# A third buffer for raw keys and queries, the fourth pair's first head placed by ScalarE, and the routing's preparations taken in turns

## The chip, the core and the metric

The kernel runs on one core of a Trainium2 chip. Its engines are TensorE (PE, with its weight loads PEld), VectorE (DVE), ScalarE (ACT) and GpSimd (POOL); SyncE (SP) issues most transfers, ScalarE some, GpSimd the gathers and scatters. Each engine works off its own list of instructions in order, and waits on semaphores for the others. The metric is device time in microseconds. The kernel before takes 926.87 us (median of 3 runs, 924.33 to 928.79).

## The reference

Causal attention with a bias over 64 heads (batch 8, 8 heads, 576 positions, head size 64), and a two-level mixture of experts on its output (4608 tokens, 4 groups of 4 experts, 512 to 1024 to 512):

```python
scores = np.matmul(q, k.transpose(0, 1, 3, 2)) / np.sqrt(D)
cum = np.cumsum(np.maximum(s, 0.0), axis=-1)
bias = -(cum[:, :, :, None] - cum[:, :, None, :])
scores = np.where(causal, -1e9, scores + np.minimum(bias, 0.0))
attn = softmax(scores)                    # over the keys
x = (attn @ v), heads joined: [4608, 512]
# then: the best group by x @ w_group, in it the best expert by x @ w_expert,
# out = (group weight * expert weight) * (relu(x @ w1) @ w2), for the tokens of each expert
```

## The kernel before

The heads are taken in 32 pairs p; a step is one head. `load_raw(p)` brings the pair's keys and queries (128 partitions by 2 by 576 floats) into a tile r of the pool raw, which has two buffers. Products are made of high and low parts: `split(p, part)` lets ScalarE copy a part of r to hl[:, part], rounded, and GpSimd subtract it from r (L155), which gives the low part. Two tiles feed TensorE. WA[p % 4] holds the high parts of both heads in rows 0 to 63, two rows of the running sum (ch or cumd), and two rows of the row maximum; WB[p % 5] holds the mixed high and low parts. Most of both is filled by transfers inside the core's memory, from hl: `load_a` (WA) and `load_b` (WB) issue them on SP. `place(p, part)` instead lets ScalarE copy straight from r: part 0 puts the first head into WA, parts 1 and 2 put two blocks into WB, and `load_a`/`load_b` with placed=True leave these transfers out. The kernel before places so for pairs 0 to 2 only.

A step runs, interleaved by an order written out by hand (`ORDER0`, `FIRST`, `ORDERS`), the row maxima of the head four steps on (A items, `rowmax`: TensorE pm, VectorE L221), the scores of its own head (B items: TensorE ps, then ScalarE's exponential L279), and the product with the values of the head before (C items: po). The scores go through a ring of three PSUM tiles, so the fourth B item waits for the exponential of the first. Letters in the order pop a queue: b is an exponential, e GpSimd's causal cut (L288), a the maximum, T and t the transposed maxima (VectorE makes th and tl, L241 and L242), D `send`, in which ScalarE issues two small transfers of th and tl into WA (L247). R calls `Router.step`, which runs the next piece of a generator in `rt.queue`, or counts down a wait that the generator yielded. The scores of pair p need the D of that pair, which comes a pair of steps before.

Before step 0 the calls are written out one after another (L456 to L514), and `pre` adds calls at the end of steps -2 to 1. From step 1 on each odd step ends with `load_a` four pairs on, `load_b` three, `load_v` one and `load_raw` six. TensorE, VectorE, ScalarE and GpSimd keep the order in which the code calls them; SP's transfers are put in order by the scheduler after step 0. Each transfer takes one of eight completion counters in turn (DMAHW0 to DMAHW7 in the instruction lists), over the queues of SP and ScalarE together, and its issue waits until the one that held its counter before, eight places ahead, has landed.

`Router.operands` (L672) makes constants for the routing: 4 memsets on GpSimd, 8 casts and small operations on VectorE. In the kernel before it is called at once at the end of step -1, so these stand between the row maxima of step -1 and those of step 0.

After attention come the lists of tokens by expert and the experts' matrix products (`moe`), whose instructions read the attention's output.

Of the kernel before, what the change touches and what calls it, by code (L numbers as in the profile page):

```python
# [8 lines left out]
F32 = mybir.dt.float32  # L9
# [10 lines left out]
B, H, S, D = 8, 8, 576, 64  # L20
P = 128
# [86 lines left out]
def attention(tc, qk, v, s, wr, xs, st):  # L108
# [3 lines left out]
    with ExitStack() as ctx:  # L112

        raw = ctx.enter_context(tc.tile_pool(name="raw", bufs=2))
# [25 lines left out]
            nc.gpsimd.memset(t[64:P, PC[4]:PC[4] + 64], 0.0)  # L140
        hls, raws = {}, {}
        def load_raw(p):
            raws[p] = raw.tile([P, 2, S], F32, name=f"r{p}", tag="r", bufs=2)
            nc.sync.dma_start(raws[p], qk[p])

        def split(p, part, later=False):

            if part == 0:
                hls[p] = raw.tile([P, 3, S], F32R, name=f"hl{p}", tag="hl", bufs=3)
            hl, r = hls[p], raws[p]  # L150
            nc.scalar.copy(hl[:, part], r[:, part])  # L151

            def low(h):
                hr = slice(0, P) if part else slice(h * 64, h * 64 + 64)
                (nc.vector if p < 1 else nc.gpsimd).tensor_tensor(  # L155
                    out=hl[:, 2] if part else WB[p % NBB][0:64, KA, h], in0=r[hr, part],
                    in1=hl[hr, part].bitcast(F32), op=ALU.subtract)

            for h in range(1 if part else 2):
                if later:  # L160
                    push("G", p, lambda h=h: low(h))
                else:
                    low(h)
# [267 lines left out]
        def need(k, i):  # L431

            while fifo[k] and fifo[k][0][0] <= i:
                pop(k)
# [22 lines left out]
        s0, r1, c2 = (c1[:BH, i * S:(i + 1) * S].bitcast(F32) for i in range(3))  # L457
        cumd = dr.tile([BH, 2, S], F32, name="cumd")
        nc.sync.dma_start(s0, s.rearrange("b h s -> (b h) s"))
        load_raw(0)  # L460
        load_raw(1)
        wr_f = ac.tile([P, 4, 20], F32, name="wr_f")
        wr_sb = ac.tile([P, 4, 40], F32R, name="wr_sb")
        nc.scalar.dma_start(wr_f, wr.rearrange("(c p) n -> p c n", p=P))
# [21 lines left out]
        XT = [ac.tile([P, 5 * 64], F32, name=f"xtl{i}") for i in range(2)]  # L486
# [8 lines left out]
        load_a(0, True)  # L495
        split(1, 0)
        split(1, 1)
        load_raw(2)
        place(0, 1)
        place(0, 2)  # L500
        place(1, 0)
# [2 lines left out]
        rt = Router(tc, ac, late, end, small, ring, wr_f, wr_sb, xs, st)  # L504
# [8 lines left out]
        for t in VT:  # L513
# [2 lines left out]

        pre = {-2: [(load_a, 2, True), (load_raw, 3), (load_v, 0)],
               -1: [(load_b, 1, True), (load_raw, 4)],
               0: [(split, 3, 0), (split, 3, 1), (load_a, 3), (load_v, 1)],
               1: [(split, 4, 0), (split, 4, 1), (load_b, 2, True), (load_raw, 5)]}  # L520
        vals, sums, pts = {}, {}, {}

# [12 lines left out]
        for step in range(-LEAD, NH + 5):  # L535
            m, a = step + LEAD, step - 1
            A = rowmax(m) if m < NH else []
            Bq, C = [], []
            if 0 <= step < NH:
                need("T", step // 2)  # L540
                need("t", step // 2)
                need("D", step // 2)
                pts[step] = PT[step % 2]
                Bq = scores(step, pts[step])
            if 0 <= a < NH:
                p = a // 2
                for k in "be":
                    need(k, a)
                if a % 2 == 0:
                    for k in "YZWK":  # L550
                        need(k, p - 2)
                    vals[p] = sm.tile([P, S], F32, name=f"vals{p}", tag="vals", bufs=2)
                    sums[p] = sm.tile([P, S], F32, name=f"sums{p}", tag="sums", bufs=2)
                C = av(a, pts.pop(a), vals[p], sums[p])
            if step >= 2 and step // 2 + 4 < NP:
                push("S", step // 2 + 4, lambda p=step // 2 + 4, part=step % 2: split(p, part, True))
            named = {"A": A, "B": Bq, "C": C}
            order = FIRST if step < 3 else ORDERS if step < NH - 1 else LAST
            for part in order[step % 2] if step > 0 else ORDER0:
                if part[0] in named:  # L560
                    for f in named[part[0]][int(part[1]):int(part[1]) + 1]:
                        f()
                elif part == "R":
                    rt.step(rt.done >= B - 2)
                elif part == "J":
                    if rt.done >= B - 2:
                        rt.step(True)
                else:
                    pop(part)
            for f, *args in pre.get(step, ()):  # L570
                f(*args)
            if step == -1:
                nc.sync.dma_start(cumd, cumh.bitcast(F32))
                rt.operands(XT)
            if step == 62:
                manual.close()
                manual.enter_context(tc.manual_schedule(engines={ENG.PE}))
            if step == 0:
                manual.close()
                manual.enter_context(tc.manual_schedule(engines={ENG.PE, ENG.DVE, ENG.Activation, ENG.Pool}))  # L580
            if step % 2 == 1 and 0 < step < NH:
                for f, lead in ((load_a, 4), (load_b, 3), (load_v, 1), (load_raw, 6)):
                    if step // 2 + lead < NP and (f != load_v or step > 1):
                        need("S", step // 2 + lead)
                        if f in (load_b, load_raw):
                            need("G", step // 2 + lead - 2 * (f == load_raw))
                        f(step // 2 + lead)
        for _ in range(3):
            for k in fifo:
                keep(k, 0)  # L590
# [37 lines left out]
class Router:  # L628


    def __init__(self, tc, ac, sm, end, ps_t, ps_s, wr_f, wr_sb, xs, st):
        self.end = end
        self.tc, self.sm, self.ps_t, self.ps_s, self.xs, self.st = tc, sm, ps_t, ps_s, xs, st
        self.wr_f, self.wr_sb = wr_f, wr_sb
        self.queue = []
        self.done = self.wait = 0
        self.logged = -1
        self.lg = {}
        nc = tc.nc
        V = nc.vector  # L640

        def iota(name, pattern, base=0, cm=0, dt=F32):
            t = ac.tile([P] + [n for _, n in pattern], dt, name=name)
            nc.gpsimd.iota(t, pattern=pattern, base=base, channel_multiplier=cm, allow_small_or_imprecise_dtypes=True)
            return t


        onesf = end.tile([P, P], F32, name="onesf", tag="rows", bufs=1)
        nc.gpsimd.memset(onesf, 1.0)
        uf = sm.tile([P, P], F32, name="uf", tag="xrt", bufs=1)  # L650
        nc.gpsimd.affine_select(out=uf, in_=onesf, pattern=[[1, P]], compare_op=ALU.is_gt, fill=0.0,
                                base=0, channel_multiplier=-1)
        self.ub = ac.tile([P, P], BF16, name="ub")
        self.ob = ac.tile([P, P], BF16, name="ob")

        self.desc = iota("desc", [[-1, 4]], base=4)
        self.real = iota("real", [[0, NB * 5], [-1, 4]], base=4)
        self.lT = ac.tile([P, 512], F32, name="lT")
        self.cols = iota("cols", [[1, P]])
        self.thr = iota("thr", [[P, NL + 1]])  # L660
        self.logit = [ac.tile([P, NB, 20], F32, name=f"logit{i}") for i in range(2)]
        for t in self.logit:
            nc.gpsimd.memset(t, 0.0)
        nc.gpsimd.memset(st.count, 0.0)
        nc.gpsimd.iota(st.ie, pattern=[[1, E]], base=0, channel_multiplier=0, allow_small_or_imprecise_dtypes=True)

        n1 = iota("n1", [[S, B], [P, NB]], base=1, cm=1, dt=I32)
        self.part = ac.tile([P, 2, B, NB], F32, name="part")
        ni = ac.tile([P, B, NB], I32, name="ni")
        self.n1, self.ni, self.uf, self.onesf = n1, ni, uf, onesf  # L670

    def operands(self, tails):  # L672
        V, ni, n1 = self.tc.nc.vector, self.ni, self.n1
        G = self.tc.nc.gpsimd
        G.memset(self.lT, 0.0)
        G.memset(self.real[64:P, 20:25], 0.0)
        for t in tails:
            G.memset(t[:, 256:320], 0.0)
        V.tensor_copy(self.wr_sb[:, :, 0:20], self.wr_f)
        V.tensor_tensor(out=self.wr_sb[:, :, 20:40], in0=self.wr_f, in1=self.wr_sb[:, :, 0:20].bitcast(F32),  # L680
                        op=ALU.subtract)
        V.tensor_copy(self.ub, self.uf)
        V.tensor_copy(self.ob, self.onesf)
        V.tensor_scalar(out=ni, in0=n1, scalar1=6, scalar2=None, op0=ALU.arith_shift_right)
        V.tensor_copy(self.part[:, 0], ni)
        V.tensor_scalar(out=ni, in0=n1, scalar1=63, scalar2=None, op0=ALU.bitwise_and)
        V.tensor_copy(self.part[:, 1], ni)

# [940 lines left out]
```

## Time and profile before

| | |
|---|---|
| median of 3 runs | 926.87 us (924.33 to 928.79) |
| the profiled execution | 922.48 us, of which the span from first to last instruction is 920.7 us |
| granted TensorE clock over the span | 0.988 of full |
| busy: PE, PEld, DVE, ACT, POOL | 854.8, 779.9, 722.3, 609.2, 606.4 us |
| share of the span | 93%, 85%, 78%, 66%, 66% |
| moved by DMA | 174.65 MB, 190 GB/s over the span |

A busy share is the mean over stages with different limits. Attention ends near 442 us and the experts follow. In the rows below, a bracket such as [0.74 <-POOL pt L288] says how long an engine sat idle before a row and what ended it; SPq and ACTq rows are issues of transfers on SP's and ScalarE's instruction streams, not the transfers themselves.

### The profile page before, as it was taken

The numbers are of one execution on the slowest core, as the hardware profiler recorded it, in microseconds if no ns is written. First come the engines' busy times: TensorE is split into PE (matmuls) and PEld (weight loads), VectorE is DVE, ScalarE is ACT, GpSimd is POOL, SyncE is SP. The second block draws the span as 40 slices with busy tenths as digits, with TensorE's granted clock in tenths as the row PEclk, the third lists the DMA queues.
The fourth block names the chain that finished last, engine by engine and source line by source line (L and its number), as shares of the span: only waits on it lengthen the run. The fifth ranks groups of instructions, "written<-read, shape, count | busy, mean of one in ns | idle before, by whom it ended". The sixth has DMA issues, their size and how long they took to land. (4 is left out here: it accounts for less than half of the span.)

```text
span 920.7 us, 17741 instructions
## 1 busy us (share of the span) xinstructions
PE 854.8 (93%) x5584; PEld 779.9 (85%) x5584; DVE 722.3 (78%) x1981; ACT 609.2 (66%) x1386; POOL 606.4 (66%) x748
## 2 busy tenths in 40 slices
PE   4879999999999999998699999999999999999995
PEld 3668788888888878886588999999999999999984
DVE  7547588797979889786467778899888899888871
ACT  5457678777777778776656566666767666767750
POOL 9656666677675768544756856766676676767650
PEclk9979999999999999999899999999999999999998
DMA  6999989999999989723635655545555555655510
GB/s 186 222 203 225 223 228 215 207 221 221 229 206 225 234 209 231 186 76 115 211 90 191 223 180 208 194 165 197 209 189 190 195 180 208 227 198 193 180 71 24
DMA packets 82165, 174.65 MB, mean 190 GB/s; under 512 B 9708, under 2 KB 45164, under 8 KB 73872
## 3 DMA queue, kind: packets, MB, share of 16 engines
q1 hardware_dynamic: 71952, 153.52, 60.2%
q0 software_dynamic: 7488, 18.89, 5.8%
q10 hardware_dynamic: 2624, 1.03, 0.5%
q8 instruction: 46, 0.75, 0.4%
q14 instruction: 55, 0.45, 0.2%
HBM read 108.97 MB, written 19.69 MB: 140 GB/s over the span
## 5 line engine op out<-in xcount | busy, mean ns | idle before, releaser
L986 POOL TENSOR_TENSOR wl<-raw,wh 128x512 fp32r<-128x512 f32 x163 | 210.2, 1304 | 68.6 <-ACT wh L983 51.8
L221 DVE CUSTOM_DVE_ANT_0 mx<-pm,mask 128x192 bf16<-128x192 f32 (+4 forms) x320 | 127.6, 419 | 41.2 <-PE pm L213 38.6
L983 ACT CAST wh<-raw 128x512 fp32r<-128x512 f32 x256 | 155.4, 616 | 1.4 <-issue 1.3
L1093 PE MATMUL ph<-xl,wh 128*128 128x256 f32 (+13 forms) x512 | 144.7, 303 | 3.1 <-DVE xl L1065 3.1
L1093 PE MATMUL ph<-xh,wh 128*128 128x256 f32 (+13 forms) x512 | 144.1, 301 | 3.3 <-ACT xh L1064 1.9
L213 PE MATMUL pm<-WA 66*128 66x288 f32 (+4 forms) x384 | 125.3, 357 | 22.2 <-DVE mc L221 11.9
L269 PE MATMUL ps<-WA 68*128 68x320 f32 (+4 forms) x384 | 136.8, 360 | 3.4 <-ACT pu L279 3.0
L309 PE MATMUL po<-pt,VT 128*128 128x256 f32 (+3 forms) x512 | 120.3, 354 | 6.5 <-ACT sums L316 3.7
L1154 PE MATMUL py<-hl,wh 128*128 128x256 f32 (+13 forms) x448 | 113.8, 303 | 1.9 <-DVE hl L1089 1.9
L1154 PE MATMUL py<-hh,wh 128*128 128x256 f32 (+13 forms) x448 | 112.8, 301 | 0.0
L271 PE MATMUL ps<-WB 128*128 128x320 f32 (+4 forms) x384 | 111.2, 302 | 0.0
L1207 DVE STREAM_TRANSPOSE yr<-yT 32x384 f32<-32x384 f32 (+1 forms) x208 | 104.5, 502 | 4.3
L309 PE MATMUL po<-pu,VT 128*128 128x320 f32 (+1 forms) x384 | 106.6, 386 | 0.3 <-POOL pu L288 0.3
L309 PEld LDWEIGHTS po<-pt,VT 128*128 128x128 f32 x512 | 88.3, 193 | 20.3 <-issue 6.2
L1060 DVE STREAM_TRANSPOSE xt<-xg 32x256 f32<-32x256 f32 (+1 forms) x208 | 102.5, 493 | 3.1
L1093 PEld LDWEIGHTS ph<-xl,wh 128*128 128x128 f32 x512 | 96.8, 189 | 5.9 <-DVE xl L1065 5.0
L1093 PEld LDWEIGHTS ph<-xh,wh 128*128 128x128 f32 x512 | 96.6, 189 | 5.4 <-ACT xh L1064 3.2
L288 POOL TENSOR_SCALAR_AFFINE_SELECT pt<-pt 128x128 f32<-128x128 f32 (+2 forms) x192 | 66.0, 355 | 49.9 <-ACT pt L279 47.4
L213 PEld LDWEIGHTS pm<-WA 66*128 66x128 f32 (+1 forms) x384 | 69.7, 193 | 32.6 <-DVE mc L221 16.1
L1088 ACT ACTIVATE hh<-ph 128x256 fp32r<-128x256 f32 (+13 forms) x128 | 53.9, 421 | 58.7 <-PE ph L1093 57.9
L155 POOL TENSOR_TENSOR WB<-r,hl 64x576 fp32r<-64x576 f32 x62 | 87.3, 1408 | 5.3 <-ACT hl L151 2.8
L1093 PE MATMUL ph<-xh,wl 128*128 128x256 f32 (+13 forms) x512 | 89.9, 299 | 0.0
(246 smaller groups left out, 1984.5 us busy)
## 6 DMA issues: line engine op xcount, KB each, us to landing
raw<-in_w_dram SPq DMA_DIRECT2D x64, 1024.0 KB
r<-in_qk_dram SPq DMA_DIRECT2D x32, 576.0 KB
WA<-hl SPq DMA_DIRECT2D x61, 288.0 KB
WB<-hl SPq DMA_DIRECT2D x61, 288.0 KB
VT<-in_v_dram SPq DMA_DIRECT2D x32, 384.0 KB
WB<-hl SPq DMA_DIRECT2D x64, 144.0 KB
xs<-xr SPq DMA_DIRECT2D x15, 512.0 KB
WA<-cumd SPq DMA_DIRECT2D x56, 4.5 KB
```

Source lines behind the costliest of these rows:

```text
L155: (nc.vector if p < 1 else nc.gpsimd).tensor_tensor(out=hl[:, 2] if part else WB[p % NBB][0:64, KA, h], in0=r[hr, part], in1=hl[hr, part]. ...
L213: nc.tensor.matmul(ps[:rows, :cw], WA[i][0:66, QA, h, QO + q0:QO + q0 + rows], WA[i][0:66, KA, h, QO + c0:QO + c0 + cw], start=True, stop= ...
L221: nc.vector.tensor_tensor_reduce(out=tmp[:rows, :cw], in0=ps[:rows, :cw], in1=mk[:rows], scale=1.0, scalar=-3.0e38 if c0 == 0 else mo, op0 ...
L269: nc.tensor.matmul(ps[:rows, o:o + w], WA[i][0:68, KA, h, QO + k0:QO + k0 + rows], WA[i][0:68, QA, h, QO + q0:QO + q0 + w], start=True, st ...
L271: nc.tensor.matmul(ps[:rows, o:o + w], WB[p % NBB][:, KA, h, k0:k0 + rows], WB[p % NBB][:, QA, h, q0:q0 + w], start=False, stop=True)
L309: nc.tensor.matmul(po[0][:, qa - base:qb - base], VT[p % NVT].rearrange("p t a d -> p (t a d)")[:, (3 * t + 1 + h) * 64:][:, 0:P], x[:, c: ...
L983: self.casts.append(nc.scalar.copy(h[:, j], raw[:, j]))
L986: self.low = lows[self.u, i, j] = nc.gpsimd.tensor_tensor(out=l[:, j], in0=raw[:, j], in1=h[:, j].bitcast(F32), op=ALU.subtract)
L1060: V.transpose(dst[:, 0:n, :, j], src[:, 0:n, :, i])
L1093: self.product = nc.tensor.matmul(pss[f][:, :cap], w[f // 4][:, c, (f % 4) * P:(f % 4 + 1) * P], x[:, c, :cap], start=(c == 0 and w is sel ...
L1154: self.product = nc.tensor.matmul(pss[c][:, :cap], w[2 + f // 4][:, f % 4, c * P:(c + 1) * P], x[:, f, :cap], start=(f == 0 and w is self. ...
L1207: V.transpose(dst[:, 0:n, :, i], src[:, 0:n, :, j])
```

## The change

The pool of raw tiles gets a third buffer, and `load_raw(2)` is called with the first two, before anything is split. Pair 3 is placed by ScalarE as pairs 0 to 2 are: three more copies at the end of step 0, between its last exponential and the first of step 1 (one of 64x2x576 into WA ahead of the two of `split`, two of 64x576 into WB behind them), one transfer of 288 KB less in `load_a(3)`, and one of 288 KB less in all in `load_b(3)`. `Router.operands` becomes a generator in the router's queue: its GpSimd part runs at the first R of step 1, then five R pass, and its VectorE part runs in five pieces at the R of step 2. `self.done` starts at -1, since one more generator is counted.

```diff
-            raws[p] = raw.tile([P, 2, S], F32, name=f"r{p}", tag="r", bufs=2)
+            raws[p] = raw.tile([P, 2, S], F32, name=f"r{p}", tag="r", bufs=3)
...
-        load_raw(0)
-        load_raw(1)
+        for p in range(3):
+            load_raw(p)
...
         split(1, 1)
-        load_raw(2)
...
-               0: [(split, 3, 0), (split, 3, 1), (load_a, 3), (load_v, 1)],
+               0: [(place, 3, 0), (split, 3, 0), (split, 3, 1), (load_a, 3, True), (place, 3, 1), (place, 3, 2), (load_v, 1)],
...
-                rt.operands(XT)
+                rt.queue.append(rt.operands(XT))
...
-                        f(step // 2 + lead)
+                        f(*((3, True) if f == load_b and step == 1 else (step // 2 + lead,)))
...
-        self.done = self.wait = 0
+        self.done, self.wait = -1, 0
...
             G.memset(t[:, 256:320], 0.0)
+        yield 5
         V.tensor_copy(self.wr_sb[:, :, 0:20], self.wr_f)
...
+        yield
         V.tensor_copy(self.ub, self.uf)
+        yield
         V.tensor_copy(self.ob, self.onesf)
+        yield
         V.tensor_scalar(out=ni, in0=n1, scalar1=6, scalar2=None, op0=ALU.arith_shift_right)
...
+        yield
         V.tensor_scalar(out=ni, in0=n1, scalar1=63, scalar2=None, op0=ALU.bitwise_and)
```

SP's transfers from the first on: cl is the input s, r0 to r2 the raw tiles, ch the running sum. Before:

```order
L459 DMA cl_126<-in_s_dram 64x576
L144 DMA r0_129<-in_qk_dram 128x1152
L144 DMA r1_131<-in_qk_dram 128x1152
L178 DMA WA0_106<-ch_125 2x1x576 [waits DVE_49,Pool_49]
L176 DMA WA0_106<-hl0_167 64x2x576 [waits Activation_49]
L178 DMA WA0_106<-ch_125 2x1x576
L144 DMA r2_182<-in_qk_dram 128x1152 [waits DMAHW2_49,DVE_49,Activation_49]
```

With the change, at the same place:

```order
L459 DMA cl_126<-in_s_dram 64x576
L144 DMA r0_129<-in_qk_dram 128x1152
L144 DMA r1_131<-in_qk_dram 128x1152
L144 DMA r2_133<-in_qk_dram 128x1152
L178 DMA WA0_106<-ch_125 2x1x576 [waits DVE_49,Pool_49]
L176 DMA WA0_106<-hl0_169 64x2x576 [waits Activation_49]
```

The load of r2 has moved ahead of three transfers and waits for nothing.

SP's transfers around the copy of the running sum to DRAM (cumd), called in step -1. Before:

```order
L144 DMA r4_346<-in_qk_dram 128x1152 [waits DMAHW1_49,Activation_49,Pool_49]
L573 DMA cumd_127<-ch_125 64x1152 [waits DMAHW2_49]
L189 DMA WB2_112<-hl2_221 64x2x576 [waits DMAHW4_49]
L189 DMA WB2_112<-hl2_221 64x576 [waits DMAHW6_49]
L178 DMA WA0_106<-cumd_127 2x576 [waits DMAHW7_49,DMAHW2_49,PE_49]
L176 DMA WA3_109<-hl3_419 64x2x576 [waits DMAHW0_49,Activation_49]
```

With the change:

```order
L144 DMA r4_346<-in_qk_dram 128x1152 [waits DMAHW0_49]
L572 DMA cumd_127<-ch_125 64x1152 [waits DMAHW1_49]
L189 DMA WB2_112<-hl2_221 64x2x576 [waits DMAHW3_49,Pool_49]
L188 DMA WB2_112<-hl2_221 64x576 [waits DMAHW5_49]
L178 DMA WA3_109<-ch_125 2x1x576 [waits DMAHW6_49,Pool_49]
L189 DMA WB2_112<-hl2_221 64x576 [waits DMAHW7_49]
L144 DMA r5_501<-in_qk_dram 128x1152 [waits DMAHW0_49,Activation_49]
L178 DMA WA0_106<-cumd_127 2x576 [waits DMAHW1_49,PE_49]
```

Between cumd's issue and the row that waits for its landing stood two transfers; now there are five, among them the load of r5, and the raw loads wait no more for GpSimd.

SP's transfers that hold the counters for which `send` of pair 3 waits (before: DMAHW6 and DMAHW7). Before:

```order
L176 DMA WA1_107<-hl5_581 64x2x576 [waits DMAHW4_49,Activation_49]
L189 DMA WB4_114<-hl4_498 64x2x576 [waits DMAHW5_49]
L192 DMA VT0_115<-in_v_dram 128x6x128 [waits DMAHW6_49,PE_49]
L188 DMA WB0_110<-hl5_581 64x576 [waits DMAHW7_49]
L176 DMA WA1_107<-hl5_581 64x2x576 [waits DMAHW0_49,PE_49]
```

With the change (DMAHW4 and DMAHW6):

```order
L176 DMA WA1_107<-hl5_582 64x2x576 [waits DMAHW3_49,Activation_49]
L192 DMA VT0_115<-in_v_dram 128x6x128 [waits DMAHW4_49,PE_49]
L144 DMA r7_672<-in_qk_dram 128x1152 [waits DMAHW5_49]
L188 DMA WB0_110<-hl5_582 64x576 [waits DMAHW6_49]
L176 DMA WA1_107<-hl5_582 64x2x576 [waits DMAHW7_49,PE_49]
```

The same two transfers hold the counters of th and tl, and the load of r7, which stood behind them, now stands between them.

## Rows read from the trace of the kernel before

**Rows 1.** Stretches of the trace (busy us by engine, clock, DMA share, GB/s)

```profile
10.00:64.60 54.60, 42.88 (x174) 33.05 (x174) 31.77 (x128) 25.05 (x54) 36.96 (x60) 0.94 0.95 217
6.50:9.50 3.00, 0.00 (x0) 0.00 (x0) 2.92 (x5) 3.00 (x6) 2.94 (x5) 1.00 0.01 3
32.00:34.00 2.00, 2.00 (x7) 1.56 (x6) 0.72 (x4) 0.75 (x2) 1.92 (x2) 1.00 0.30 65
...
100.00:390.00 290.00, 279.10 (x1784) 241.46 (x1785) 238.01 (x842) 216.63 (x543) 198.96 (x308) 1.00 0.92 218
```

**Rows 2.** TensorE's rows in time that end a pause (start, us, instruction, [idle before])

```profile
26.09 0.53 PE L213 MATMUL pm<-WA 66*128 66x192 f32 x1 [2.44 <-DVE mc L221]
...
43.66 0.70 PE L309 MATMUL po<-pt,VT 128*128 128x256 f32 x2 [0.74 <-POOL pt L288]
...
46.02 0.38 PE L269 MATMUL ps<-WA 68*128 68x256 f32 x1 [1.04 <-ACT pu L279]
...
49.10 0.63 PE L269 MATMUL ps<-WA 68*128 68x320 f32 x1 [1.92 <-ACT pu L279]
...
64.60 0.67 PE L309 MATMUL po<-pt,VT 128*128 128x256 f32 x2 [3.67 <-ACT sums L316]
```

**Rows 3.** ScalarE's stream in time, at the two late issues of row maxima

```profile
44.66 0.72 ACTq L247 DMA_DIRECT2D WA<-tl  x1
45.43 0.54 ACT L279 ACTIVATE pu<-ps 128x448 f32<-128x448 f32 x1 [4.52 <-PE pm L213]
...
62.51 0.75 ACTq L247 DMA_DIRECT2D WA<-th  x1
...
64.13 0.38 ACT L316 ACTIVATE sums<-po 64x256 f32<-64x256 f32 x1 [5.27 <-DMA WA<-th]
```

**Rows 4.** VectorE's rows in time: th and tl made for those two issues

```profile
39.33 0.28 DVE L242 SCALAR_TENSOR_TENSOR tl<-pmt,th 10x128 fp32r<-10x128 f32 x1
...
57.83 0.28 DVE L242 SCALAR_TENSOR_TENSOR tl<-pmt,th 10x128 fp32r<-10x128 f32 x1
```

**Rows 5.** DMA issues by kind on the page (count, KB each)

```profile
r<-in_qk_dram SPq DMA_DIRECT2D x32, 576.0 KB
WA<-hl SPq DMA_DIRECT2D x61, 288.0 KB
WB<-hl SPq DMA_DIRECT2D x61, 288.0 KB
```

**Rows 6.** SP's stream in time: r2, cumd, and the wait for cumd

```profile
10.42 0.34 SPq L144 DMA_DIRECT2D r<-in_qk_dram  x1
...
24.53 0.47 SPq L573 DMA_DIRECT2D cumd<-ch  x1
...
31.94 0.27 SPq L178 DMA_DIRECT2D WA<-cumd  x1
```

**Rows 7.** ScalarE's stream in time: placing of pair 2, first exponentials of step 1

```profile
14.67 1.15 ACT L167 CAST WA<-r 64x1152 fp32r<-64x1152 f32 x1 [1.84 <-DMA r<-in_qk_dram]
...
16.88 1.34 ACT L167 CAST WB<-r 64x576 fp32r<-64x576 f32 x2
...
30.62 0.48 ACT L279 ACTIVATE pt<-ps 64x64 f32<-64x64 f32 x2
```

**Rows 8.** VectorE's rows in time: first, third and last of the eight preparations

```profile
21.51 0.72 DVE L679 CAST wr_sb<-wr_f 128x80 fp32r<-128x80 f32 x1
...
22.43 1.05 DVE L682 CAST ub<-uf 128x128 bf16<-128x128 f32 x1
...
25.48 0.47 DVE L687 CAST part<-ni 128x40 f32<-128x40 int32 x1
```

**Rows 9.** GpSimd's subtractions of pair 4, in time

```profile
38.81 2.88 POOL L155 TENSOR_TENSOR WB<-r,hl 64x576 fp32r<-64x576 f32 x2 [2.43 <-ACT hl L151]
41.77 1.40 POOL L155 TENSOR_TENSOR hl<-r,hl 128x576 fp32r<-128x576 f32 x1
```

**Rows 10.** The two stretches with the clock at half

```profile
48.57:55.39 6.82, 6.29 (x21) 5.28 (x21) 2.02 (x10) 2.64 (x8) 3.92 (x6) 0.50 1.03 210
65.63:69.05 3.42, 3.42 (x17) 3.37 (x16) 1.73 (x5) 3.32 (x9) 1.23 (x1) 0.50 0.73 185
```

## The prediction

> **What bounds the kernel now.** I read the stretches first: GB/s and PE's share over time. From 10 to 64.6 us DMA is busy 95% of the time and moves 217 GB/s, while PE works 42.88 of 54.60 us; from 100 to 390 us PE works 279.10 of 290 [rows 1]. So the place where anything can be gained is the first 65 us; what is late there shifts all that follows, since the experts read the attention's output.
>
> Next come PE's pauses in that stretch: 2.44 us at 26.09 behind VectorE, 0.74 at 43.66 behind GpSimd, 1.04 at 46.02 and 1.92 at 49.10 behind ScalarE's exponentials, and 3.67 at 64.60 behind ScalarE's sums [rows 2]. Third, why ScalarE is late. Its stream is in order, and the issues of `send` stand in it. VectorE has tl of pair 2 ready at 39.61 us and that of pair 3 at 58.11 [rows 4]; ScalarE issues the first at 44.66, 5.05 us later, and can't issue th of the second before 62.51, 4.40 us after both were there, and everything behind it stands: 4.52 and 5.27 us of idling [rows 3]. What they wait for is a completion counter, held by the transfer eight places ahead: by the order of issue VT0 and WB0 for the second of these stops. Transfers that are issued run one behind another. So the two stops end when the DMA has moved the bytes ahead, and in the head of this kernel the DMA sets the pace.
>
> **The change part by part.** The working is a sum over bytes: what is moved into time in which the DMA stands idle, and how many bytes stand ahead of the second stop.
>
> The early load of r2. Between 6.5 and 9.5 us the DMA moves 3 GB/s [rows 1]: r0 and r1 are there, and the first WA transfers wait for VectorE's running sum. Before, r2 is issued at 10.42 and ScalarE's copy that reads it starts at 14.67, 1.84 us late [rows 6, 7]; it then stands in the busy stream. Now it fills the slot. 576 KB [rows 5] are 0.59 MB; at 217 GB/s the stream loses 2.7 us of work. The bounds: 4.25 us (10.42 to 14.67, the whole passage of r2), and 0, if its tail keeps the first WA transfers waiting as long as it saves. I take 2.7.
>
> The pause of SP at cumd. WA0<-cumd reads what cumd<-ch has written, and SP can issue nothing behind it until that has landed: cumd is issued at 24.53, the reader at 31.94 [rows 6]. Only two transfers stand between, and the DMA runs dry: 65 GB/s from 32 to 34 us [rows 1]. Now five stand between, among them r5 with 576 KB, so this dry stretch goes: 2 us x (1 - 65/217) = 1.4 us. The bounds are 0 (it runs dry at a later wait for ScalarE's split of pair 3) and 2.
>
> Bytes ahead of the second stop. `load_a` of pair 3 saves a transfer of 288 KB and `load_b` 288 KB in all [rows 5]. Against that, the raw loads are one pair further ahead: r7 now stands in front of the WB0 whose counter tl takes. Ahead of tl it is -576 + 576 = 0 KB, so nothing here. The kinds differ (raw loads come from outside the core, the others copy inside it); if one is a quarter faster, 0.7 us either way. In the first stop only half of that has been added, and it comes earlier still; but what PE wins there it stands waiting for at the second, which the same bytes end.
>
> VectorE's preparations. They run from 21.51 to 25.95, 4.44 us, in front of the maxima [rows 8], and PE pauses 2.44 us [rows 2]. With them gone PE reaches step 1 about 2.4 us sooner, and ScalarE's `send` of pair 1 with it. They come back in step 2, in five pieces between maxima, and GpSimd's memsets in step 1. At nothing, since the first stop, still there, covers them: th isn't let out before its counter is free. Without that cover they cost up to 4.4.
>
> The copies of pair 3: 1.15 + 1.34 = 2.49 us on ScalarE [rows 7], in front of step 1's exponentials, which began at 30.62. PE comes 2.4 us sooner, ScalarE stays where it was: at nothing, up to 2.5 us if PE runs out of score tiles.
>
> Here the skill speaks against the change. A cast of 128x128 on VectorE took 1.05 us [rows 8], and in step 2 GpSimd is at its three subtractions of pair 4, 2.88 + 1.40 us [rows 9]. The Trainium skill (SBUF — State Buffer, section "Who interferes with whom") says that casts and such on VectorE and GpSimd's operations can lock each other out of a shared port for a whole instruction. By that rule the preparations could take 4.3 us longer in step 2 and the sum would be 926.87 - 4.1 + 4.3 = 927.1 without cover; the rows of before don't show the two kinds side by side, and with the stop as cover the sum stays.
>
> The sum is 2.7 + 1.4 + 0 = 4.1 us. From 100 us on I change nothing: PE works 96% of that stretch [rows 1], and the third buffer moves loads that nobody waits for there. The profiled execution took 922.48 us, so 918.4 on its scale; it is 4.4 us under the median of the runs, 926.87, from which the same sum gives **922.8 us**.
>
> **The rivals.** A: the stops go altogether. If ScalarE's counters are no longer late, all pauses of [rows 2] fall away, 2.44 + 0.74 + 1.04 + 1.92 + 3.67 = 9.8 us, and with them the clock at half, 6.82 and 3.42 us at 1.2 of 2.4 GHz [rows 10], of which half is lost, 5.1 us: 14.9 us together, 912.0. For it: three of the five pauses are ScalarE's, and the clock falls behind each of the two stops. Against it: 217 GB/s is also what moves from 100 to 390 us [rows 1], so the DMA has no more to give, and the bytes ahead of the second stop are the same. The Trainium skill (TensorE: Matmul & The Clock Gate, section "HAM oscillation — how this bites in real kernels") has it that pauses behind transfers throttle TensorE and that closing them keeps it fast; the trace agrees as to the fall [rows 10]. My forecast keeps one long pause, and so the loss.
>
> B: nothing is won. r2's last bytes hold up the first WA transfers as long as the slot saves (0 in place of 2.7 us), and 576 KB of raw loads take 1.4 us longer than the 576 KB of copies inside the core that they stand in for, which eats the dry stretch: 4.1 - 2.7 - 1.4 = 0, 926.9. For it: r2 took 4.25 us on its way before, more than 2.7. Against it: it shared the stream then with what was issued around it, and the slot is 3 us wide [rows 1].
>
> C, slower: ScalarE becomes the bound in step 1. Its three copies stand in front of the exponentials; if these start more than 2 us after 30.62 [rows 7], the ring of three score tiles stops TensorE, GpSimd's cuts follow late, and if the bytes aren't what ends the later stops the 2.49 us stay: 929.4. Against it: `send` of pair 1, which stands in front of step 0's last exponentials and waits for VectorE, comes sooner with VectorE, and the stops behind are longer than 2.49 us [rows 3].
>
> **How the numbers follow.** The forecast has 0.55, its own range 920.5 to 925 (sum between 1.9 and 6.4); A 0.15, from 917 down to 910; B 0.22, 925 to 928; C 0.08, 928 to 934. About 0.5% (4.6 us, the line at 922.2) is what a measurement of this kernel can tell from no change. Of the forecast 0.42 lies below it: 0.23, with A 0.38 for faster. Slower is the upper part of C, and a little for what shifts in the experts' part: 0.05. The rest, 0.57, is the same. The range of eight in ten leaves out most of A and of C: 917 to 928.
>
> **What would show it.** Right: DMA above 150 GB/s from 6.5 to 8 us, ScalarE's copy of r2 no later than 13 us with no idling in front; no stretch near 65 GB/s before 40 us; no pause of PE near 24; `send` of pair 2 let out near 40 and that of pair 3 near 59 to 60, with a longer idling of ScalarE in front of it than 5.27; attention's end some 4 us sooner, and the distance from there to the end unchanged. Wrong: th and tl issued as soon as VectorE has made them (A), the second stop where it was (B), PE waiting for ScalarE in step 1 and the raw loads early without use (C), or a difference that appears only behind 440 us.

## The result and the profile after

| | before | with the change |
|---|---|---|
| median of 20 runs | 928.24 us (921.58 to 935.18) | 921.65 us (916.19 to 928.71) |
| ratio, with its 95% interval | | 0.9914 (0.9891 to 0.9937) |
| the same again, in e11 | | 0.9913 (0.9883 to 0.9943) |
| span of the profiled run | 920.7 us | 917.1 us |

The kernel is 0.86% faster by the ratio, some 8 us; the two medians stand 6.6 us apart. The forecast, 922.8 us against 926.87, was a ratio of 0.9956: right in sign and with the time inside its range, but the gain is twice the 4.1 us of the sum, and 0.9956 lies outside the interval. That the median lies within 1.2 us of 922.8 is in part luck: the kernel before stood at 926.87 us by three runs and stands at 928.24 by twenty, and 0.9914 of 926.87 would be 918.9, below the forecast's own 920.5 to 925, though inside its 917 to 928. A gain of more than 0.5% had 0.38 of its chances, no telling difference 0.57. The spans of the two profiled runs differ by 3.6 us only; each is one draw from a spread of 12 to 14 us, and that of before, 922.48 us, lies below all but one of its 20.

The stretches of [rows 1], and two more, after the change (busy us by engine, clock, DMA share, GB/s):

```profile
6.50:9.50 3.00, 0.00 (x0) 0.00 (x0) 2.78 (x5) 3.00 (x5) 2.94 (x4) 1.00 0.49 200
10.00:64.60 54.60, 46.94 (x226) 37.89 (x227) 37.12 (x146) 35.82 (x77) 41.80 (x69) 1.00 0.92 235
...
32.00:34.00 2.00, 2.00 (x8) 1.61 (x7) 0.83 (x4) 1.84 (x6) 1.85 (x3) 1.00 0.85 239
...
100.00:390.00 290.00, 278.90 (x1770) 241.91 (x1769) 239.66 (x849) 212.76 (x533) 195.91 (x303) 0.99 0.84 212
...
48.57:55.39 6.82, 6.82 (x46) 6.00 (x44) 4.63 (x20) 3.90 (x9) 5.26 (x8) 1.00 1.04 265
...
45.00:60.00 15.00, 13.07 (x84) 11.44 (x83) 10.86 (x39) 10.43 (x25) 9.37 (x14) 1.00 1.02 256
```

The slot at 6.5 us is filled and the stretch at 65 GB/s is gone. In the head PE works 46.94 us in place of 42.88, at full clock throughout, also in the stretch that stood at half [rows 10]. And the DMA, called full at 217 GB/s, moves 235. From 100 to 390 us little has changed; PE's clock there is 0.99, before 1.00.

TensorE's first row and its pauses of over 0.8 us before 65 us, after the change [rows 2]:

```profile
9.99 0.95 PE L213 MATMUL pm<-WA 66*128 66x288 f32 x3 [9.99 <-DMA WA<-ch]
...
24.25 0.55 PE L269 MATMUL ps<-WA 68*128 68x256 f32 x1 [3.28 <-DMA WA<-tl]
...
46.37 0.35 PE L213 MATMUL pm<-WA 66*128 66x192 f32 x1 [1.11 <-DVE mc L221]
...
56.64 0.67 PE L309 MATMUL po<-pt,VT 128*128 128x256 f32 x2 [0.82 <-issue]
```

Of the five pauses of before, those behind VectorE's preparations, behind GpSimd and behind ScalarE's exponentials are gone, the last fell from 3.67 to 0.82 us. There are two new ones: 1.11 us behind VectorE, and 3.28 us in front of the first scores, where PE waits for the tl of pair 0.

ScalarE's stream, after [rows 3 and 7]:

```profile
13.44 1.15 ACT L167 CAST WA<-r 64x1152 fp32r<-64x1152 f32 x1
...
41.37 1.30 ACTq L247 DMA_DIRECT2D WA<-tl  x1
42.72 0.54 ACT L279 ACTIVATE pu<-ps 128x448 f32<-128x448 f32 x1 [1.79 <-PE po L309]
...
52.72 0.75 ACTq L247 DMA_DIRECT2D WA<-th  x1
...
55.40 0.73 ACTq L247 DMA_DIRECT2D WA<-tl  x1
56.17 0.38 ACT L316 ACTIVATE sums<-po 64x256 f32<-64x256 f32 x1 [2.55 <-DVE mc L221]
...
59.69 0.58 ACT L404 COPY xr<-px 128x512 f32<-128x512 f32 x1
```

and VectorE's tl for those two issues [rows 4]:

```profile
40.56 0.28 DVE L242 SCALAR_TENSOR_TENSOR tl<-pmt,th 10x128 fp32r<-10x128 f32 x1
...
52.72 0.28 DVE L242 SCALAR_TENSOR_TENSOR tl<-pmt,th 10x128 fp32r<-10x128 f32 x1
```

The copy of r2 waits for nothing. The first stop is gone (tl made at 40.84, its issue begun at 41.37; before, 5.05 us late), and of the second, th goes out as it is made and tl 2.4 us after it is made, where both waited over 4 us.

SP's stream, after [rows 6]:

```profile
1.47 1.51 SPq L144 DMA_DIRECT2D r<-in_qk_dram  x3
...
22.34 0.60 SPq L572 DMA_DIRECT2D cumd<-ch  x1
...
30.19 0.28 SPq L178 DMA_DIRECT2D WA<-cumd  x1
```

The three raw loads go out together, and the reader of cumd comes 1.75 us sooner than before.

In what follows the yardstick for the head is the distance from PE's first instruction to ScalarE's first copy xr, since the arrival of the first inputs, and VectorE's work on them, differ by up to 2 us between runs. Before:

```profile
9.70 0.95 PE L213 MATMUL pm<-WA 66*128 66x288 f32 x3 [9.70 <-DMA WA<-ch]
```

```profile
67.65 0.58 ACT L404 COPY xr<-px 128x512 f32<-128x512 f32 x1
```

That is 57.95 us before, and 59.69 - 9.99 = 49.70 after: the head gives 8.25 us, about the 8 us of the ratio.

Behind attention a part of it is lost again. From the start of PE's last product with the values to the end it is 479.4 us before and 481.3 after (483.0 in e11). The seven profiles with the third buffer stand at 481.3 to 483.0, and e7 (below), with a spare tile of the same size, at 482.4; the five without either (before, e2, e3, e6, e12) at 478.7 to 479.7. One place of the loss shows in the rows: a small operation of VectorE that came ahead of GpSimd's subtractions before comes beside them now. VectorE before:

```profile
473.69 0.42 DVE L1315 TENSOR_TENSOR sel<-rank,ie 128x256 bf16<-128x256 f32 x1
```

VectorE after, and GpSimd:

```profile
475.91 7.61 DVE L1319 TENSOR_TENSOR sel<-rank,ie 128x256 bf16<-128x256 f32 x1
```

```profile
471.52 7.51 POOL L990 TENSOR_TENSOR wl<-raw,wh 128x512 fp32r<-128x512 f32 x6
479.48 3.76 POOL L990 TENSOR_TENSOR wl<-raw,wh 128x512 fp32r<-128x512 f32 x3
```

It takes 7.61 us in place of 0.42 and ends as GpSimd's second run ends; PE, behind it, idles 3.02 us for VectorE at 485.77. In e1, e5 and e7 it is two operations, 3.39 and 4.17 us, for 0.42 each before. Why a larger pool of raw tiles moves the order there, no run shows.

### The profile page after: what moved, and what is told of

Its sections match the earlier page's. It is cut to its first block, busy times and chain, and to the rows that moved or that the text cites. A ratio compares the mean times of both kernels' runs of the same rounds, so it can differ in the third digit from the quotient of the medians.

```text
span 917.1 us, 17750 instructions
## 1 busy us (share of the span) xinstructions
PE 852.1 (93%) x5584; PEld 778.8 (85%) x5584; DVE 730.3 (80%) x1981; ACT 611.0 (67%) x1389; POOL 606.0 (66%) x748
## 4 chain that ended last, share of the span: by engine, by line
PE 65%; DVE 17%; ACT 7%; issue 6%; DMA 4%; POOL 1%; POOLq 0%; ACTq 0%; DVEq 0%; SPq 0%
PE po L309 17%; PE ph L1097 14%; PE py L1158 13%; PE pm L213 6%; PE ps L271 5%; PE ps L269 5%; DVE yr L1211 3%; DVE xt L1064 2%; ACT wh L987 2%; DMA out_dram<-yT,ids 2%; DVE hl L1093 2%; DVE wl L997 2%; PE px L398 2%; ACT pw L995 1%; DVE mx L221 1%
## 5 line engine op out<-in xcount | busy, mean ns | idle before, releaser
L371 POOL TENSOR_TENSOR xTl<-xT,xTh 128x512 fp32r<-128x512 f32 x30 | 38.3, 1275 | 79.9 <-ACT xTh L367 59.8
```

## The experiments

Each kernel was timed in five rounds beside the kernel before on its chip, but for e9. The yardstick comes from one profile each; for the kernel before and two variants that win nothing (e7, e12) it is 57.95, 57.27 and 58.31, for the change twice 49.70 and 50.36, so a difference below 1 us says nothing.

| | buffer | placed | turns | yardstick, us | ratio to before (95%) |
|---|---|---|---|---|---|
| before | | | | 57.95 | 1 |
| e1 | x | | | 54.20 | 0.9946 (0.9917 to 0.9976) |
| e2 | | x | | 55.47 | 0.9938 (0.9905 to 0.9971) |
| e3 | | | x | 54.74 | 0.9964 (0.9929 to 0.9999) |
| e4 | x | x | | 50.56 | 0.9929 (0.9898 to 0.9961) |
| e5 | x | | x | 53.11 | 0.9935 (0.9905 to 0.9965) |
| e6 | | x | x | 52.60 | 0.9948 (0.9913 to 0.9984) |
| change | x | x | x | 49.70 | 0.9914 (0.9891 to 0.9937) |

### e1 to e3: one part alone

e1, against the kernel before:

```diff
-            raws[p] = raw.tile([P, 2, S], F32, name=f"r{p}", tag="r", bufs=2)
+            raws[p] = raw.tile([P, 2, S], F32, name=f"r{p}", tag="r", bufs=3)
...
-        load_raw(0)
-        load_raw(1)
+        for p in range(3):
+            load_raw(p)
...
-        load_raw(2)
```

> Only the third raw buffer and the early load of r2. Yardstick: start of the first copy xr of ScalarE, 67.65 us before, 59.69 after. Bytes (the forecast's reckoning): 2.7 us from the early slot and 1.4 from the dry stretch, less 2.7 for the 576 KB of r7 that now stand in front of the second stop: xr near 66.2, tl of pair 3 let out about 62, time ratio 0.998. Waits of SP (rival): the raw loads no more wait for GpSimd, so SP runs ahead and both stops shrink without the other parts: xr near 61, ratio 0.993. Clock (rival): the remainder of the 8 us is the clock at half, which stays as long as a stop of over 3 us stays: both falls still there, xr no earlier than 65.

e2:

```diff
-               0: [(split, 3, 0), (split, 3, 1), (load_a, 3), (load_v, 1)],
+               0: [(place, 3, 0), (split, 3, 0), (split, 3, 1), (load_a, 3, True), (place, 3, 1), (place, 3, 2), (load_v, 1)],
...
-                        f(step // 2 + lead)
+                        f(*((3, True) if f == load_b and step == 1 else (step // 2 + lead,)))
```

> Only pair 3's first head placed by ScalarE. Bytes: 576 KB less in front of the second stop, 2.7 us: xr near 65.0, ratio 0.997; the dry stretch near 33 us stays. Waits of SP: raw loads still wait for GpSimd, so little: xr 67 or later, ratio 1.0. Clock: one of the two falls may go with 2.7 us, then xr near 62.

e3:

```diff
-                rt.operands(XT)
+                rt.queue.append(rt.operands(XT))
...
-        self.done = self.wait = 0
+        self.done, self.wait = -1, 0
...
+        yield 5
         V.tensor_copy(self.wr_sb[:, :, 0:20], self.wr_f)
...
+        yield
```

> Only the preparations taken in turns. Bytes: no byte less; the wait for cumd has seven transfers in front of it by the instruction lists, so the dry stretch goes: at most 1.4 us, xr 66.3 to 67.7, ratio 0.9985 to 1.0. VectorE (rival): the 4.44 us of preparations stood on the path, and PE's pause at 26.09 with them: 2.4 us or more, xr 65 or earlier, ratio 0.997.

The placing wins 2.48 us on the yardstick, as its bytes say. The buffer wins 3.75 where the bytes gave 1.4, and the turns, which save no byte, 3.21. The 3.75 may be too high: PE starts at 11.52 us in e1, 1.8 us later than before, so counted from the start of the span its xr comes only 1.93 us sooner. By time the three are not told apart. In e3 the DMA's stretch from 26 to 40 us, in which before stood the dry 2 us:

```profile
26.00:40.00 14.00, 13.73 (x62) 11.36 (x63) 8.13 (x31) 7.89 (x20) 9.72 (x17) 1.00 1.06 262
```

and the same of before:

```profile
26.00:40.00 14.00, 13.89 (x60) 11.57 (x61) 6.91 (x34) 7.63 (x19) 7.95 (x15) 1.00 0.86 218
```

In e1 it is 1.04 and 242 GB/s. So each of these two parts alone keeps the DMA at work there, by a fifth of 14 us, 2.8 us. Two explanations were left for e3: SP's wait for cumd, 3.3 us in the waits of before and none in e3, or VectorE.

### e4 to e6: two parts

The diffs are those above put together.

> Third buffer and placing, preparations where they were. Bytes: the whole sum, 4.1 us: xr near 63.5, ratio 0.996. Waits of SP or clock: nearly all of the change's gain, xr 60 to 61, ratio 0.992. VectorE: 2.4 us less than the change, xr near 62.1.

> Third buffer and turns, pair 3 not placed. Yardstick: distance from PE's first instruction to the first copy xr (57.95 us before, 49.70 after; 54.20 with the buffer alone, 54.74 with the turns alone). If the two win different waits they add up: 51.0, ratio 0.991. If both fill the same dry stretch behind cumd (1.4 us by the forecast): 52.4. If it is one and the same stop that either of them removes: 54, ratio 0.995.

> Placing and turns, two raw buffers. The same yardstick (placing alone 55.47, turns alone 54.74). If they add up: 52.3, ratio 0.991. If it is one stop that either removes: 54.5, ratio 0.995. The raw loads still wait for GpSimd here, so r7 stands behind the transfers that hold the counters of pair 3: th and tl should leave together, within 1 us.

Placing adds 2.1 to 3.6 us whatever stands beside it. Buffer and turns win 4.84 us together and 6.96 apart by the yardstick, but from the start of the span 4.87 together and 1.93 + 3.09 apart: whether they overlap is not shown. Nor do the two together fill the dry stretch. In e5, and in the change, the DMA from 26 to 40 us is hardly busier than the 0.86 before, though it moves more:

```profile
26.00:40.00 14.00, 13.83 (x63) 11.57 (x63) 7.11 (x28) 8.17 (x20) 8.42 (x16) 1.00 0.88 232
```

```profile
26.00:40.00 14.00, 13.68 (x64) 11.47 (x63) 7.37 (x30) 10.44 (x23) 8.13 (x15) 1.00 0.86 249
```

With buffer and placing there the turns bring 0.2 to 0.9, inside the noise. In e6 th and tl of pair 3 leave within 1 us of each other (57.10 and 57.94), in e4, where r7 stands between their counters' holders, 4.1 apart (51.46 and 55.58).

### e7: the addresses

```diff
+        pad = raw.tile([P, 2, S], F32, name="pad", tag="pad", bufs=1)
+        nc.gpsimd.memset(pad[:, 0, 0:1], 0.0)
```

> The kernel before with a spare tile of 4608 bytes per partition in the pool of raw tiles, of which GpSimd clears one column; no transfer reads or writes it. If the new addresses in the on-chip memory make the DMA faster (rival to all reasons from order): DMA from 45 to 60 us at 240 GB/s or more in place of 205, yardstick 54 or less. If not: 205 GB/s, yardstick 58, ratio 1.0; this also shows how far one profile stands from another.

From 45 to 60 us the DMA moves 216 GB/s, the yardstick is 57.27, the ratio 1.0051 (1.0017 to 1.0084). Shifted addresses alone bring nothing. The whole is slower by 0.5%, 4.7 us; 3.0 of them stand behind attention in its profile, the loss shown above (482.4 us for 479.4).

### e9: what a byte costs

```diff
+    with ExitStack() as ctx:
+        spare = ctx.enter_context(tc.tile_pool(name="spare", bufs=1))
+        xt = [spare.tile([P, 2, S], F32, name=f"x{i}", tag=f"x{i}", bufs=1) for i in range(12)]
+        for i in range(24):
+            nc.sync.dma_start(xt[i % 12], qk[i])
+        yt = [spare.tile([P, 2, QW], F32, name=f"y{i}", tag=f"y{i}", bufs=1) for i in range(12)]
+        for i in range(48):
+            nc.sync.dma_start(yt[i % 12][0:64, :, QO:], xt[i % 12][64 * (i % 2):64 * (i % 2) + 64])
```

> The kernel before with a measuring stretch in front: 24 raw loads of 576 KB into spare tiles (14.2 MB), then 48 copies of 288 KB (14.2 MB) of 64 partitions by 2 by 576 inside the on-chip memory, all on SP's queue; attention follows behind them, so its time is not compared. The forecast counted both kinds at 217 GB/s. If a byte costs the same in either, both stretches show the same rate and r7 in front of pair 3's tl is paid for by the copies that placing saves. Rival: raw loads move at 330 to 350 GB/s and copies at 200 to 215, as stretches of 2 us suggest (341 where r7 passes, 203 where copies alone pass): then the swap of 576 KB is worth 1.1 to 1.2 us.

The stretch of raw loads, and that of copies:

```profile
8.00:28.00 20.00, 0.00 (x0) 0.00 (x0) 1.74 (x2) 0.00 (x0) 0.00 (x0) 1.00 1.02 401
44.00:104.00 60.00, 0.00 (x0) 0.00 (x0) 0.00 (x0) 0.00 (x0) 0.00 (x0) 1.00 1.04 200
```

Each kind alone, a byte copied inside the core costs two of a load from outside; the share of DMA is full in both. 576 KB (0.59 MB) of copies are 2.9 us, 576 KB of raw loads 1.5 us. So 217 GB/s said nothing about a limit: it is a mixture, with idle time in it. Mixed, as in the head, the two prices lie nearer together: from 6 us to the first xr the trace's records of DMA packets have 269 ns for a packet of a raw load (one row, 4608 bytes) and 169 for one of a copy (2304 bytes) before, 224 and 155 after the change, where e9 has 186 and 190. Spread over 16 engines, 576 KB of raw loads are then 2.2 us before and 1.8 after, 576 KB of copies 2.7 and 2.5.

### e12: the wait for cumd alone

```diff
+            if step == -2:
+                nc.sync.dma_start(cumd, cumh.bitcast(F32))
             if step == -1:
-                nc.sync.dma_start(cumd, cumh.bitcast(F32))
                 rt.operands(XT)
```

> The kernel before with one edit: the write of cumd is called a step earlier, so that seven transfers (1872 KB by the instruction lists) in place of two stand between it and the first row that waits for it; buffers, placing and the preparations are as before. If SP's wait of 3.3 us for cumd is what the turns and the third buffer take away: that wait gone, yardstick (PE's first instruction to first xr; 57.95 before) 54.5 to 55, as with the turns alone (54.74), while PE's pause behind the preparations (2.44 us at 26.09) stays; ratio 0.9965. If the turns win through VectorE instead: yardstick 57 to 58, ratio 1.0.

The wait is gone, and nothing is won: yardstick 58.31, ratio 1.0011 (0.998 to 1.0042). SP's stream in e12:

```profile
28.82 0.39 SPq L178 DMA_DIRECT2D WA<-cumd  x1
30.75 0.62 SPq L176 DMA_DIRECT2D WA<-hl  x1
32.85 0.65 SPq L178 DMA_DIRECT2D WA<-ch  x1
```

and the DMA in it from 26 to 40 us:

```profile
26.00:40.00 14.00, 13.55 (x59) 11.36 (x60) 7.18 (x35) 7.58 (x19) 8.08 (x16) 1.00 0.87 208
```

The reader of cumd goes 3.1 us sooner than at 31.94 [rows 6], and the next row, the copy of hl3, waits for ScalarE's split of pair 3, which starts at 29.48 as before (29.46). The dry stretch only moved behind it (137 GB/s from 34 to 36 us). In e3 it is the split that comes sooner, since VectorE makes the row maxima of pair 1 sooner. VectorE's row, and ScalarE's, in e3:

```profile
23.38 0.28 DVE L242 SCALAR_TENSOR_TENSOR tl<-pmt,th 10x128 fp32r<-10x128 f32 x1
```

```profile
26.30 1.24 ACT L151 CAST hl<-r 128x576 fp32r<-128x576 f32 x2
```

Before:

```profile
26.26 0.28 DVE L242 SCALAR_TENSOR_TENSOR tl<-pmt,th 10x128 fp32r<-10x128 f32 x1
```

```profile
29.46 1.24 ACT L151 CAST hl<-r 128x576 fp32r<-128x576 f32 x2
```

These are 2.88 and 3.16 us later. That fits the turns' 3.21 us: preparations, maxima, `send` of pair 1, the exponentials in order behind it, the split, and only then the DMA. It is argued from these times, and the wait for cumd had to go as well: in e3 SP issues the copies of hl3 ahead of the reader of cumd:

```profile
28.47 1.17 SPq L176 DMA_DIRECT2D WA<-hl  x1
...
32.90 0.48 SPq L178 DMA_DIRECT2D WA<-cumd  x1
```

With the old order, hl3 would have stood behind the reader. Taking away the wait for cumd alone wins nothing (e12); sooner maxima alone, in the old order, no run shows.

### e8 and e10: the stops that are left

e8, the changed kernel with r7 held behind the transfers into WB0:

```diff
+            if step == 5:
+                behind(tc, load_raw(7), wbq[5, 0])
```

Here wbq[5, 0] is the first transfer of load_b(5), and the call of load_raw(7) at the end of step 3 is left out.

> The changed kernel with the load of r7 held behind the transfers into WB0 (a dependency on one queue, no semaphore). Bytes: 432 KB less stand in front of the transfer that holds the counter of tl of pair 3, 1.3 to 2 us at 341 to 217 GB/s: tl let out near 53.7 in place of 55.40, within 1 us of th, ScalarE's idling before it 1 us in place of 2.55, yardstick 48.2. If the DMA's rate comes from raw loads that stand between the copies inside the core: rate from 45 to 60 us falls from 256 toward 205 and nothing is won. Ratio to the kernel before 0.990 or, without a gain, 0.991.

ScalarE in e8, at the `send` of pair 3:

```profile
54.93 0.75 ACTq L247 DMA_DIRECT2D WA<-th  x1
...
55.77 0.72 ACTq L247 DMA_DIRECT2D WA<-tl  x1
56.55 0.38 ACT L316 ACTIVATE sums<-po 64x256 f32<-64x256 f32 x1 [0.72 <-DVE mc L221]
```

The second stop is gone, so r7 was what held tl. But the yardstick is 50.86: in this profile the new pause in front of the first scores was 4.90 us and took the gain. From 45 to 60 us its DMA moved 235 GB/s, between the 256 of the change and the 205 that the expectation names for the case that raw loads between copies make the rate.

e10, e8 with r3 and VT0 behind the three transfers into WB1:

```diff
-        pre = {-2: [(load_a, 2, True), (load_raw, 3), (load_v, 0)],
-               -1: [(load_b, 1, True), (load_raw, 4)],
+        pre = {-2: [(load_a, 2, True)],
+               -1: [(load_b, 1, True), (load_raw, 3), (load_v, 0), (load_raw, 4)],
```

> The kernel of e8 with r3 and VT0 called behind the three transfers into WB1: 432 KB in place of 960 KB then stand in the queue in front of th and tl of pair 0, which PE awaits 3.28 us at 24.25 in the changed kernel and 4.90 in e8. Bytes: 528 KB less, 1.5 us at 341 GB/s to 2.5 at 217: PE's first scores near 22, yardstick 48 (49.70 for the change, 50.86 for e8), ratio to before 0.988. If the stops of pair 2 and 3 end by bytes alone, the win comes back there: tl of pair 2 or 3 late again by 1 us or more, yardstick 50.

PE's first scores in e10:

```profile
21.57 0.55 PE L269 MATMUL ps<-WA 68*128 68x256 f32 x1 [0.92 <-DMA WA<-tl]
```

The pause fell to 0.92 us and the yardstick to 46.95, the lowest of all. Later it is given back in part: the fourth xr stands 83.02 us behind PE's first instruction, in the change 83.01 in one profile and 87.33 in the other. By time e8 stands at 0.9899 (0.9858 to 0.9940) and e10 at 0.9892 (0.9846 to 0.9938) of the kernel before: the best two, but not told apart from the change.

### e11: the change again

> The changed kernel once more, for its spread and beside e10: yardstick 49 to 51, ratio to before 0.991.

Yardstick 50.36, ratio 0.9913 (0.9883 to 0.9943). From 70 to 100 us its DMA moved 221 GB/s where the first profile shows 243, by the same program: beyond 60 us, single profiles of one kernel stand 4 us apart.

## Why the prediction was right, and where it failed

**Which part bounds.** Right: the gain comes in the first 65 us, 8.25 us by the yardstick, and the steady part up to 390 us stays. "The third buffer moves loads that nobody waits for there" held up to the end of attention only: behind it stands a loss of 1.9 to 3.6 us, a cost that the sum lacks.

**The rate, the step that failed first.** "217 GB/s is also what moves from 100 to 390 us, so the DMA has no more to give" took a rate for a limit. By e9 the kinds stand 401 to 200, and the same queue moved 235 in the head. Two terms hang on it. "Bytes ahead of the second stop: -576 + 576 = 0, 0.7 us either way" is +2.9 - 1.5 = 1.4 us, an estimate from the rates of e9, and 0.6 to 0.7 by the packets of the head, which is the forecast's "0.7 us either way"; on the one side e2 measures 2.48. The early load of r2, 2.7 us, is 1.5 by e9, 1.8 to 2.2 by the packets. It did what was said: the slot at 200 GB/s, the copy at 13.44 without idling (the sign said 13).

**The dry stretch.** It was priced at 1.4 us from a window of 2 us and put down to cumd. e12 takes the wait for cumd away and wins nothing; the bound named beside it, that SP next waits for the split of pair 3, is what happens. With the turns alone (e3) or the buffer alone (e1) the DMA works through it; in e5 and in the change it does not (shares of 0.88 and 0.86). The 4.84 us of e5 are measured, but this stretch does not explain them.

**VectorE's preparations at nothing.** Wrong for them alone: 3.21 us in e3. As the times of e3 and e12 have it, the first stop, named as their cover, is itself ended by transfers that wait for VectorE through ScalarE. Beside the other two parts, nearly right. Their return in step 2 cost nothing that shows. The rule of the Trainium skill (SBUF — State Buffer, section "Who interferes with whom") was weighed at 4.3 us; in step 2 the casts do stand beside GpSimd's subtractions. VectorE's cast of ub, and GpSimd, after the change [rows 8 and 9]:

```profile
38.91 1.42 DVE L683 CAST ub<-uf 128x128 bf16<-128x128 f32 x1
```

```profile
38.84 2.89 POOL L155 TENSOR_TENSOR WB<-r,hl 64x576 fp32r<-64x576 f32 x2 [1.85 <-ACT hl L151]
41.80 1.41 POOL L155 TENSOR_TENSOR hl<-r,hl 128x576 fp32r<-128x576 f32 x1
```

GpSimd's are as long as before (2.88 and 1.40), the cast is 0.37 us longer. So in step 2 no more than some tenths are seen. Behind attention it is otherwise: there VectorE's `sel` took 7.61 us beside GpSimd for 0.42 ahead of it.

**The new sum**: 4.84 as e5 measured it for buffer and turns and 2.9 for the placed copies by e9, 7.7 of the 8.25 us. It says which part brought what, not how. The DMA's queue from the start of the span to the first xr (packets, MB, share of 16 engines), before (0 to 67.65 us) and after (0 to 59.69):

```profile
q1 hardware_dynamic: 7428, 13.55, 84.3%
```

```profile
q1 hardware_dynamic: 7295, 13.54, 83.9%
```

The same bytes kept it busy for 57.0 us before and for 50.1 after, while its idle time fell by 1.0 us only. So what shrank is for the most part not idle time, as the forecast had it, but the time that packets took; the swap of kinds explains 0.6 to 1.4 us of that. A raw load's packet took 254 ns in e1 and 261 in e3, 234 in e4 and 245 in e5 (269 before, 266 and 270 in e7 and e12, 224 and 230 in the two profiles of the change). What shortens them is open; shifted addresses alone (e7) do not.

**Signs.** Attention ended 5.6 us sooner, for some 4, but the distance from there to the end did not stay. Wrong was "no pause of PE near 24": the pause behind VectorE is gone, but SP now runs ahead and puts r3 and VT0, 960 KB, into the queue in front of the small transfers of pair 0. e10 moves them and the pause goes. Wrong was also "a longer idling than 5.27" at pair 3: 2.55.

**The rivals.** A had more truth than its 0.15: the first stop goes, the clock in the head is full (1.00 for 0.94), only tl of pair 3 still waits. But its 5.1 us of clock are not all kept. Over all runs the mean of span times granted clock, an estimate of the span at full clock, is 910.8 us before (31 runs beside e1 to e4) and 905.8 with the change (its 20 runs): 5.1 us gone. The mean spans are 8.2 apart, so some 3.1 are clock. Later in attention the clock may fall or not behind one and the same pause. Of before, PE and the 3.4 us behind the pause:

```profile
240.94 0.74 PE L213 MATMUL pm<-WA 66*64 66x64 f32 x2 [1.77 <-DVE mc L221]
```

```profile
240.90:244.30 3.40, 3.32 (x17) 2.72 (x18) 3.20 (x11) 2.34 (x6) 0.23 (x1) 1.00 0.59 114
```

and the like row of the kernel after, four pairs later (at the same place of the program, 232.21 us, the pause is 1.76 us too):

```profile
283.22 1.02 PE L213 MATMUL pm<-WA 66*64 66x64 f32 x2 [1.76 <-DVE mc L221]
```

```profile
283.20:286.60 3.40, 3.38 (x8) 2.46 (x9) 2.42 (x8) 1.67 (x5) 0.23 (x1) 0.50 0.34 115
```

The same pause leaves the clock at 2.4 GHz in one and at 1.2 in the other; such a fall costs half of its 3.4 us, and runs of the change have mean clocks from 0.981 to 0.990. In the two profiled runs it is 0.988 both times, so there nothing of the clock is kept. B is refuted by the slot and by e1, and its raw loads cost less than copies, not more (e9). C did not come: ScalarE's placing stands at 28.84 and the exponentials of step 1 begin at 32.42, 1.8 us later than at 30.62 [rows 7], which PE did not wait for.

Open: why the same transfers move at 221 or 243 GB/s from 70 to 100 us in two runs of one program, why packets of the head take less time with the change, and why a larger pool of raw tiles moves VectorE's `sel` beside GpSimd.

## What to carry to other kernels

A DMA stream is full only against the rate of its own kinds of transfers; measure each kind by itself before a mixed rate is read as a limit, price the bytes that are swapped by kind, and then look at what a packet takes in the mixture. A wait that ends last is not what it costs: take it away alone, and see whether the next one in the same queue stands at the same time. A cover that is itself ended by the work it is to hide is no cover. And follow a change to the end of the program: a buffer added for the head went with a loss of some 3 us behind attention.

## What the runs showed of the hardware

Copies of 64 partitions with rows of 2304 bytes inside the on-chip memory moved 200 GB/s, loads of 128 rows of 4608 bytes from outside 401 GB/s, both with the DMA's share full (1.04 and 1.02). Their packets took 190 and 186 ns there, and in the mixture of the head 154 to 173 and 224 to 272. An operation of VectorE (128x256, two inputs) took 7.61 us beside GpSimd's subtractions and 0.42 ahead of them. A transfer of 5 KB issued on ScalarE's queue was usable the later the more stood already in SP's: tl of pair 0 was issued at 18.22 and PE could read it at 24.25 with 960 KB of loads ahead, and in e10, issued at 17.91, at 21.57.
